# Heads of odd units change sides in the values' products, and the first two experts are picked by early counts

## The chip, the cores and the metric

The kernel runs on one core of one Trainium2 chip. The metric is the device time of one execution in microseconds; the median of three runs is compared. Five engines work side by side: TensorE (matrix products; "PE" in the rows, "PEld" for its weight loads), VectorE ("DVE"), ScalarE ("ACT"), GpSimd ("POOL") and SyncE ("SP", which here only sends DMAs). A "q" behind an engine's name means its instruction queue.

## The reference

Three layers follow each other on 2304 tokens (4 batches of 576) of width 512.

```python
# attention, 8 heads of 64: a down-sampled branch over groups of 4 tokens, and a local band
out_d  = softmax(q4 @ k4.T / 8) @ v4            # q4, k4, v4: means over 4 tokens
out_up = repeat(out_d, 4)
mask   = abs(i - j) < 4
x = out_up + softmax(where(mask, q @ k.T / 8, -1e9)) @ v
# gated layer, d_ff 1536
x = (silu(x @ w_gate) * (x @ w_val)) @ w_out
# 8 experts, d_ff 1024: each token goes to one
e = argmax(cosine(x, expert_emb) / tau);  p = softmax(...)[e]
out = p * (relu(x @ w1[e]) @ w2[e])
```

## The kernel before

**Order.** The kernel is written as some hundred generator tasks. A planner in Python (`Sched`) runs them at build time: each `yield op(engine, ns, priority)` asks for an engine for an estimated time, `wait` and `get` wait for events and buffers, and the planner picks by priority and estimated time which task emits its instructions next. What comes out is a fixed instruction order per engine. Priorities are constants (`HEAD_P`, `WEIGHT_P`, `ROW_P`, ...); `LAT` is the time that the planner allows from one engine to the next.

**Attention.** Work goes by head pairs n = 0 to 15 (batch b = n // 4). The two heads of a pair lie in partitions 0 to 63 and 64 to 127. A sequence is cut into NU = 10 units of UQ = 58 queries; a unit's band needs 64 keys. Pairs 0 to 3 take tasks of their own (`local_e`, `down_e`, `piece_e`). Pairs 4 to 15 take `scores` (band scores, unit u of head h2 into bank `lp[h2]`, even units in the lower and odd units in the upper 64 partitions), `local` (softmax), and `values`: transposes of the weights, the down-sampled product into `av`, then 20 products of 64x64 by 64x58, one for each unit and head, into two banks, 464 columns into the first. `up` is a copy of `av`; VectorE adds `up` to the products into x32, at chunk borders and at the bank's end. With f32 operands each such product stands as two records in the trace.

**Gated layer.** x32 holds chunks of 256 tokens in NX = 3 buffers; `x_split` cuts each into a high and a low part, and products are done in three parts (high by high, high by low, low by high). Chunks are worked on in order 0 to 8; 2 and 3, and 4 and 5, go together.

**Routing.** After a chunk's last product, `route_rows` and `first_rows` multiply its rows by the eight expert rows on VectorE, `route` finds the expert of each token and its place among that expert's tokens, with the counts so far in `base`; `route_base` adds the chunk's counts. GpSimd scatters token numbers into a table in memory (`tab`).

**Experts.** Each expert has a fixed number of slots by its place in the order (`CAPS`; 336 slots are three tiles of 128, 128 and 80). Expert 0 always comes first (`FIXED = 1`); its weights are loaded once the products of chunk 7 are issued, and its first 256 slots are filled from chunks 0 to 7. The others are ranked by their final counts (`last_base`), after chunk 8, and their numbers are loaded into registers from `ordi` (`set_order`, line 1460); `load_experts`, `load_slots` (line 1699: table, line 1720: gather) and `load_groups` (gathers from the third expert on) wait for "turns". Should an expert have more tokens than slots, a block at the end of the kernel handles the rest.

```python
            if e == FIXED:
                yield ("wait", "turns")
```

## Time and profile before

| what | before |
|---|---|
| median of 3 runs | 811.74 us (811.62 to 813.75) |
| profiled execution | 808.81 us, its span 807.2 us |
| TensorE busy | 789.4 us (98%) |
| VectorE busy | 563.2 us (70%) |
| ScalarE busy | 369.1 us (46%) |
| GpSimd busy | 195.1 us (24%) |
| mean granted TensorE clock | 0.997 |

The profiled execution is one run of its own; its span goes from the first to the last instruction. Matmuls are pipelined, so a record's time is longer than the distance to the next one, and the distance of starts tells the pace. Records in one row of the timeline are merged.

### The profile page before, as it was taken

Reading aid. Unit: us, or ns where it says so; the run is one execution under the profiler, and the core shown is the slowest. Engines: PE = TensorE matmul, PEld = TensorE weight load, DVE = VectorE, ACT = ScalarE, POOL = GpSimd, SP = SyncE. Lnnn points to the kernel's source line nnn. Section 1 sums busy time; section 2 is a strip of 40 time slices with the busy share of each in tenths; the row PEclk is TensorE's granted clock in tenths of the full one; section 3 lists DMA queues with packets and bytes.
Section 4 is the critical chain, followed back from the end, with each engine's and each line's share of the span. In section 5 each row is a group of like instructions: output and inputs, shape, how many; then the busy total and the mean of one; then the engine's idle time right before and its main releaser. Section 6 shows DMA issues by size and latency. Waiting matters only on the chain. (4 is left out here: it accounts for less than half of the span.)

```text
span 807.2 us, 16215 instructions
## 1 busy us (share of the span) xinstructions
PE 789.4 (98%) x6122; PEld 691.1 (86%) x6128; DVE 563.2 (70%) x1472; ACT 369.1 (46%) x919; POOL 195.1 (24%) x208
## 2 busy tenths in 40 slices
PE   8989999999999999999999999999989999999997
PEld 5778778877877877877899999999979999999996
DVE  5899889768755468656399997675568778657620
ACT  3887788662332261232241312335345555545531
POOL 5533300010000010000013312012357163555201
PEclk9999999999999999999999999999999999999999
DMA  8995255512201112201143010052189666676401
GB/s 248 283 285 169 63 202 183 166 66 88 75 1 61 62 65 88 75 1 61 67 131 62 19 41 1 27 149 87 29 237 275 217 198 189 180 221 191 156 14 42
DMA packets 64371, 96.35 MB, mean 119 GB/s; under 512 B 15085, under 2 KB 34031, under 8 KB 64160
## 3 DMA queue, kind: packets, MB, share of 16 engines
q1 hardware_dynamic: 59424, 85.50, 34.9%
q0 software_dynamic: 4576, 9.51, 4.0%
q8 instruction: 49, 0.80, 0.4%
q14 instruction: 34, 0.28, 0.1%
q10 hardware_dynamic: 288, 0.26, 0.1%
HBM read 85.42 MB, written 10.29 MB: 119 GB/s over the span
## 5 line engine op out<-in xcount | busy, mean ns | idle before, releaser
L1176 PE MATMUL ps<-xb,w 128*128 128x512 f32 x512 | 171.9, 398 | 0.0
L1120 PE MATMUL ps<-xb,w 128*128 128x256 f32 x960 | 128.1, 285 | 0.3 <-ACT w L726 0.3
L1120 PEld LDWEIGHTS ps<-xb,w 128*128 128x128 f32 x960 | 121.8, 191 | 2.2 <-ACT w L726 0.5
L1176 PEld LDWEIGHTS ps<-xb,w 128*128 128x128 f32 x512 | 96.1, 188 | 22.4 <-issue 0.8
L1851 PE MATMUL ps<-xh,w 128*128 128x288 f32 (+4 forms) x512 | 111.2, 299 | 0.2
L1176 PE MATMUL ps<-xl,w 128*128 128x512 f32 x256 | 100.6, 393 | 0.0
L1851 PEld LDWEIGHTS ps<-xh,w 128*128 128x128 f32 x512 | 84.9, 188 | 1.2 <-ACT sg L1921 1.0
L1647 DVE TENSOR_TENSOR w<-w,w 128x1024 fp32r<-128x1024 f32 x64 | 76.6, 1217 | 8.2 <-ACT w L1644 7.5
L1851 PE MATMUL ps<-xl,w 128*128 128x288 f32 (+4 forms) x256 | 75.9, 296 | 0.0
L1792 POOL DMA_INDIRECT xs<-x2d,w x55 | 64.1, 1166 | 23.0 <-issue 14.3
L1644 ACT CAST w<-w 128x1024 fp32r<-128x1024 f32 x64 | 65.9, 1050 | 0.0
L1835 ACT ACTIVATE eh<-ps 128x288 fp32r<-128x288 f32 (+4 forms) x62 | 26.0, 419 | 83.9 <-PE ps L1851 73.7
L1837 DVE SCALAR_TENSOR_TENSOR el<-ps,eh 128x288 fp32r<-128x288 f32 (+4 forms) x62 | 28.0, 456 | 51.7 <-ACT eh L1835 51.2
L1176 PEld LDWEIGHTS ps<-xl,w 128*128 128x128 f32 x256 | 48.2, 188 | 8.7
L1238 PE MATMUL x<-w,hh 128*128 128x512 f32 x160 | 50.2, 395 | 0.0
L1851 PEld LDWEIGHTS ps<-xl,w 128*128 128x128 f32 x256 | 48.2, 188 | 0.2
L1957 PE MATMUL x<-eh,w 128*128 128x288 f32 (+3 forms) x192 | 46.8, 301 | 0.0
L1957 PE MATMUL ps<-eh,w 128*128 128x288 f32 (+3 forms) x192 | 46.8, 301 | 0.0
L1135 ACT ACTIVATE th<-ps 128x256 f32<-128x256 f32 x64 | 21.1, 380 | 50.8 <-PE ps L1176 50.8
L1150 ACT CAST hh<-th 128x256 fp32r<-128x256 f32 x64 | 24.1, 407 | 39.8 <-DVE th L1144 39.5
L1208 PE MATMUL x<-w,hh 128*128 128x512 f32 x128 | 41.2, 403 | 0.0
L1137 DVE SCALAR_TENSOR_TENSOR th<-th,ps 128x256 f32<-128x256 f32 x64 | 24.1, 415 | 24.5 <-ACT th L1135 24.3
(343 smaller groups left out, 1691.6 us busy)
## 6 DMA issues: line engine op xcount, KB each, us to landing
w<-w SPq DMA_DIRECT2D x64, 512.0 KB
w<-w_gate SPq DMA_DIRECT2D x10, 512.0 KB
w<-w_val SPq DMA_DIRECT2D x10, 512.0 KB
w<-w_out SPq DMA_DIRECT2D x10, 512.0 KB
aw<-qk SPq DMA_DIRECT2D x16, 291.0 KB
x2d<-sg SPq DMA_DIRECT2D x18, 256.0 KB
w<-qk SPq DMA_DIRECT2D x12, 291.0 KB
xl<-x2d SPq DMA_DIRECT2D x13, 256.0 KB
```

The costliest lines, as they stand in the source:

```text
L1120: nc.tensor.matmul(ps[:, o:o + CT], ww[:, k, fs], xx[:, k, :], start=(k == 0 and n == 0), stop=(k == KD - 1 and n == 2))
L1137: nc.vector.scalar_tensor_tensor(out=th, in0=th, scalar=1.0, in1=pg[:, r], op0=ALU.add, op1=ALU.mult)
L1176: nc.tensor.matmul(ps, ww[:, k, fs], xx[:, :, k], start=(k == 0 and n == 0), stop=(k == KD - 1 and n == 2))
L1208: nc.tensor.matmul(x2p[x], l, r[:, js], start=(u == 0 and n == 0), stop=(u == 2 * NFB - 1 and n == 2))
L1238: nc.tensor.matmul(x2p[c, m], l[:, j, ms], r[:, js], start=(p == 0 and j == 0 and n == 0), stop=(p == NFB - 1 and j == 1 and n == 2))
L1644: nc.scalar.copy(hi.bitcast(F32R), raw)
L1647: nc.vector.tensor_tensor(out=lo.bitcast(F32R), in0=raw, in1=hi.bitcast(F32R), op=ALU.subtract)
L1792: nc.gpsimd.indirect_dma_start(out=xs[:, n * P:(n + 1) * P], out_offset=None, in_=x2d.rearrange("t (a d) -> (t a) d", a=KD), in_offset=bas ...
L1835: nc.scalar.activation(hh[:, j, 0:n].bitcast(F32R), ps[:, 0:n], AF.Relu)
L1837: nc.vector.scalar_tensor_tensor(out=hl[:, j, 0:n].bitcast(F32R), in0=ps[:, 0:n], scalar=0.0, in1=hh[:, j, 0:n].bitcast(F32R), op0=ALU.max ...
L1851: nc.tensor.matmul(ps[:, 0:n], ww[:, k, fs], xx[:, k, 0:n], start=(k == 0 and t == 0), stop=(k == KD - 1 and t == 2))
L1957: nc.tensor.matmul(ys[d][:, 0:n], ww, h, start=(f == 0 and t == 0), stop=(f == NF2 - 1 and t == 2))
```

## The change

Three things change. In `scores`, odd units of the two heads go to the other bank, so that in the weights' transposes odd units have the heads' rows swapped; V's odd units are swapped to fit in the layout on the host (pairs 4 to 15). In `values` a product of an odd unit then reads the other half of the rows than it writes of the columns, and the products of even units go to one bank and those of odd units to the other. x32 becomes one ring of three chunks, into which VectorE adds by bank, in the pieces that `runs` gives; `up` is written with each column twice.

The first two experts are picked by `pick`: the one with the highest count behind chunk 6, and behind chunk 7 the highest of the others. `set_one` loads their numbers into registers on SyncE and GpSimd. The other six are ranked after chunk 8 as before. The second place has 312 slots in place of 336.

All priorities and latencies of the planner are new.

```diff
 EARLY = 256
-FIXED = 1
-CAPS = (CAP, CAP, 312, 304, 288, 288, 288, 256)
+CAPS = (CAP, 312, 312, 304, 288, 288, 288, 256)
 SLTE = [tuple(m for m in (P, P, n - 2 * P) if m) for n in CAPS]
...
 NT18 = NTOK // P
-NRK = E - FIXED
+NRK = E
 NCST = P + P // 2 + NPAIR * WK // 2 + 3 * E + 4 * NT18 + NOV + NRK
...
 DMA_T = 700.0
-ACT_P, XP_P, ROW_P, FIRST_P = -0.456, 0.525, -0.154, 30.295
+ACT_P, XP_P, ROW_P, FIRST_P = -0.496, 0.501, 3.222, -1.474
 NX = 3
...
 
-    LAT = {"PE": 210.0, "DVE": 158.0, "ACT": 178.0, "POOL": 143.0}
-    LAT_DMA = 4951.0
+    LAT = {"PE": 210.0, "DVE": 196.0, "ACT": 216.0, "POOL": 181.0}
+    LAT_DMA = 4954.0
     ENTER, LEAVE = 90.0, 240.0
...
 
-HEAD_P = [-2.038, -0.549, -1.624, -1.708, 2.951, 3.075, 1.758, 4.264, 14.859, 18.007, 17.102, 19.186, 33.984, 40.93, 39.946, 38.167]
+HEAD_P = [-3.109, 0.648, -2.052, -1.667, 2.606, 4.218, 1.43, 4.125, 17.975, 14.873, 18.249, 18.867, 37.092, 43.121, 42.894, 40.716]
 NE = 8
...
 NV = 4
-REST_P = [-0.295, -0.252, 0.316, 2.344]
-HALF_P = [0.379, -1.498, 1.707, 0.836]
-VALUE_P = 0.832
-PART_P = [-0.851, 0.298, 0.473]
-CONST_P = 7.293
-TAB_P = 13.08
-EN_P = 0.425
+REST_P = [0.348, 0.116, 0.229, 4.192]
+HALF_P = [-5.803, -4.869, 2.17, 0.149]
+VALUE_P = 1.151
+PART_P = [-0.006, 0.163, 0.799]
+CONST_P = 6.238
+TAB_P = 10.974
+EN_P = 1.384
 EN_T = 0.0
...
 UH = NU // 2
-WEIGHT_P = [1.273, 2.395, 4.193, 0.175, -6.884, 9.779]
+WEIGHT_P = [1.883, 3.305, 7.321, 0.411, -8.772, 3.174]
 
...
     ordi = cst.tile([P, NRK], I32, name="ordi")
-    nc.gpsimd.memset(cape, float(CAP))
+    one = cst.tile([P, 4], F32, name="one")
+    onei = cst.tile([P, 2], I32, name="onei")
+    floor = cst.tile([P, E], F32, name="floor")
 
...
     left = [6 * NFB]
-    slots("x32", atp, NX, [P, KD, CT], True)
+    ring = atp.tile([P, KD, NX * CT], F32, name="ring")
+    for i in range(NX):
+        sc.slots["x32"].append((0.0, ring[:, :, i * CT:(i + 1) * CT]))
     slots("xl2", atp, 1, [P, 2 * KD * CT], True)
...
             t0 = unit0(u)
-            for h2, s in enumerate(lp):
-                nc.tensor.matmul(s[(u % 2) * 64:(u % 2) * 64 + 64, u // 2 * WK:(u // 2 + 1) * WK],
+            for h2 in range(2):
+                nc.tensor.matmul(lp[(h2 + u) % 2][(u % 2) * 64:(u % 2) * 64 + 64, u // 2 * WK:(u // 2 + 1) * WK],
                                  sq[row(h2), t0:t0 + 64], sk[row(h2), t0:t0 + WK], start=True, stop=True)
...
         eT = sk[:GH, 0:4 * G].rearrange("p (h g) -> p h g", h=2)
-        up = sq[:, SP6 + 2 * G:SP6 + 3 * G]
-        xa, xb = yield from pget(2)
-        av = xb[:, 256:256 + G]
+        up = sq[:, SP6:SP6 + 2 * G]
+        xp = yield from pget(2)
+        av = xp[1][:, NPAIR * UQ + 10:NPAIR * UQ + 10 + G]
         yield ("lag", SLACK)
-        yield op("PE", 490 + 20 * 52 + 90, None, "s")
+        yield op("PE", 490 + 10 * 64 + 90, None, "s")
         for kh in range(2):
...
                                  start=(kh == 0), stop=(kh == 1))
-        cut = 8 * UQ
         for u in range(NU):
...
             i = u // 2 * P % 256 + u % 2 * 64
-            xp, q = (xa, UQ * u) if UQ * u < cut else (xb, UQ * u - cut)
+            q = u // 2 * UQ
             for h2 in range(2):
-                r = slice(h2 * D, (h2 + 1) * D)
-                nc.tensor.matmul(xp[r, q:q + UQ - o], sv[r, u * D:(u + 1) * D], T[u // 4][r, i + o:i + UQ], start=True, stop=True)
-        eng = yield psum(G)
-        copy[eng](up, av)
-        t0 = 0
-        while t0 < S:
-            c, o = divmod(b * S + t0, CT)
-            e = min(S, t0 + CT - o, cut if t0 < cut else S)
-            xp, q = (xa, t0) if t0 < cut else (xb, t0 - cut)
-            yield op("DVE", t_dve(e - t0), -1.0)
-            nc.vector.tensor_tensor(
-                out=x32[c][:, hp, o:o + e - t0].rearrange("p (g f) -> p g f", f=4),
-                in0=xp[:, q:q + e - t0].rearrange("p (g f) -> p g f", f=4),
-                in1=up[:, t0 // 4:e // 4].unsqueeze(2).to_broadcast([P, (e - t0) // 4, 4]), op=ALU.add)
-            x_left[c, hp] -= e - t0
+                r, d = ((h2 + u) % 2 * D, h2 * D)
+                nc.tensor.matmul(xp[u % 2][d:d + D, q:q + UQ - o], sv[r:r + D, u * D:(u + 1) * D], T[u // 4][r:r + D, i + o:i + UQ],
+                                 start=True, stop=True)
+        eng = yield psum(2 * G)
+        copy[eng](up.rearrange("p (g f) -> p g f", f=2), av.unsqueeze(2).to_broadcast([P, G, 2]))
+        for e in range(2):
+            for m, us, t0, t1 in runs(b, e):
+                k = (t1 - t0) // 2
+                at_ = (b * S + t0) % (NX * CT)
+                yield op("DVE", t_dve(2 * m * k), -1.0)
+                nc.vector.tensor_tensor(
+                    out=ap_of(ring, (hp * NX * CT + at_), [[2 * UQ, m], [2, k], [1, 2]]),
+                    in0=ap_of(xp[e], us // 2 * UQ + t0 - UQ * us, [[UQ, m], [2, k], [1, 2]]),
+                    in1=ap_of(up, t0 // 2, [[UQ, m], [1, k], [0, 2]]), op=ALU.add)
+            if e == 0:
+                pput(xp[0])
+        pput(xp[1])
+        for c in range(b * S // CT, (b * S + S - 1) // CT + 1):
+            x_left[c, hp] -= min(b * S + S, (c + 1) * CT) - max(b * S, c * CT)
             if x_left[c, hp] == 0:
                 sc.set(("xr", c, hp))
-            if e in (cut, S):
-                pput(xa if e == cut else xb)
-            t0 = e
         sc.set(("done", n))
+
+    def runs(b, e):
+
+        cut = -(b * S) % (NX * CT)
+        got = []
+        for u in range(e, NU, 2):
+            t0, t1 = UQ * u, min(UQ * (u + 1), S)
+            for a, z in ((t0, min(t1, cut)), (max(t0, cut), t1)) if t0 < cut < t1 else ((t0, t1),):
+                if got and a == t0 and z - a == UQ and got[-1][3] - got[-1][2] == UQ and not (got[-1][2] < cut <= a):
+                    got[-1][0] += 1
+                else:
+                    got.append([1, u, a, z])
+        return got
 
...
         for c in range(NCHUNK):
-            x32[c] = yield ("get", "x32")
+            yield ("get", "x32")
+            x32[c] = ring[:, :, c % NX * CT:(c % NX + 1) * CT]
             sc.set(("x32", c))
...
         nc.vector.tensor_tensor(out=base, in0=base, in1=base0, op=ALU.subtract)
-        r0, lo = iota8[:, 0, 0:NRK], iota8[:, 0, FIXED:]
+        r0 = lo = iota8[:, 0, :]
         key, rank, val = rk[:, 0], rk[:, 1], rk[:, 2]
...
         yield op("DVE", 75, -0.9, True)
-        nc.vector.scalar_tensor_tensor(out=key, in0=lo, scalar=-1.0 / 16, in1=base[:, FIXED:], op0=ALU.mult, op1=ALU.add)
+        nc.vector.scalar_tensor_tensor(out=key, in0=lo, scalar=-1.0 / 16, in1=base, op0=ALU.mult, op1=ALU.add)
+        yield op("DVE", 75, -0.9, True)
+        nc.vector.tensor_tensor(out=key, in0=key, in1=rk[:, 3], op=ALU.add)
         yield op("DVE", 110, -0.9, True)
...
         yield op("DVE", 100, -0.8)
-        nc.vector.tensor_reduce(out=cape[:, FIXED:], in_=rk2, axis=AX.X, op=ALU.add)
+        nc.vector.tensor_reduce(out=cape, in_=rk2, axis=AX.X, op=ALU.add)
         yield op("DVE", 75, -0.8, True)
...
         yield ("lag", 500)
-        for i in range(NRK):
-            on_ = [mybir.EngineType.SP] + ([mybir.EngineType.Pool] if FIXED + i == 1 else [])
-            turn[FIXED + i] = nc.values_load(ordi[0:1, i:i + 1], engines=on_, min_val=FIXED, max_val=E - 1,
-                                             skip_runtime_bounds_check_because="a permutation of the ranked experts")
+        for i in range(2, E):
+            turn[i] = nc.values_load(ordi[0:1, i:i + 1], engines=[mybir.EngineType.SP], min_val=0, max_val=E - 1,
+                                     skip_runtime_bounds_check_because="a permutation of the ranked experts")
         sc.set("turns")
...
 
-        return x[e] if e < FIXED else x[bass.ds(turn[e], 1)].rearrange("o r c -> (o r) c")
+        return x[bass.ds(turn[e], 1)].rearrange("o r c -> (o r) c")
 
...
 
-            yield op("DVE", 75, -0.9)
-            nc.vector.tensor_scalar(out=base[:, 0:1], in0=base[:, 0:1], scalar1=float(EARLY), scalar2=None, op0=ALU.max)
+            yield ("wait", "picked")
+            yield op("DVE", 75, -0.9, True)
+            nc.vector.tensor_tensor(out=base, in0=base, in1=floor, op=ALU.max)
+        if c >= NCHUNK - 3:
+            sc.spawn(sc.cur.prio, pick(c - NCHUNK + 3))
         sc.set(("base", c))
+
+    def pick(i):
+
+        key, up_, got = rk[:, 0], rk[:, 2], rk[:, 3]
+        lo = iota8[:, 0, :]
+        yield op("DVE", 75, -0.7, True)
+        nc.vector.tensor_tensor(out=key, in0=base, in1=base0, op=ALU.subtract)
+        yield op("DVE", 75, -0.7, True)
+        nc.vector.scalar_tensor_tensor(out=key, in0=lo, scalar=-1.0 / 16, in1=key, op0=ALU.mult, op1=ALU.add)
+        if i == 1:
+            yield op("DVE", 75, -0.7, True)
+            nc.vector.tensor_tensor(out=key, in0=key, in1=got, op=ALU.subtract)
+        yield op("DVE", 80, -0.7)
+        nc.vector.tensor_reduce(out=one[:, i:i + 1], in_=key, axis=AX.X, op=ALU.max)
+        yield op("DVE", 75, -0.7, True)
+        nc.vector.tensor_scalar(out=up_, in0=key, scalar1=one[:, i:i + 1], scalar2=None, op0=ALU.is_equal)
+        yield op("DVE", 75, -0.7, True)
+        nc.vector.tensor_tensor(out=key, in0=up_, in1=lo, op=ALU.mult)
+        yield op("DVE", 80, -0.7)
+        nc.vector.tensor_reduce(out=one[:, 2 + i:3 + i], in_=key, axis=AX.X, op=ALU.add)
+        yield op("DVE", 75, -0.7, True)
+        nc.vector.tensor_copy(onei[:, i:i + 1], one[:, 2 + i:3 + i])
+        sc.set(("one", i))
+        if i == 0:
+            yield op("DVE", 75, -0.7, True)
+            nc.vector.scalar_tensor_tensor(out=floor, in0=up_, scalar=float(EARLY), in1=base0, op0=ALU.mult, op1=ALU.add)
+            yield op("DVE", 75, -0.7, True)
+            nc.vector.tensor_scalar(out=got, in0=up_, scalar1=8192.0, scalar2=None, op0=ALU.mult)
+            sc.set("picked")
+        else:
+            yield op("DVE", 75, -0.7, True)
+            nc.vector.scalar_tensor_tensor(out=got, in0=up_, scalar=4096.0, in1=got, op0=ALU.mult, op1=ALU.add)
+
+    def set_one(i):
+
+        yield ("wait", ("one", i))
+        yield ("lag", 500)
+        turn[i] = nc.values_load(onei[0:1, i:i + 1], engines=[mybir.EngineType.SP, mybir.EngineType.Pool], min_val=0, max_val=E - 1,
+                                 skip_runtime_bounds_check_because="the place of a maximum among the experts")
+        sc.set(("turn", i))
 
...
         for e in range(E):
-            if e == FIXED:
-                yield ("wait", "turns")
+            yield ("wait", ("turn", e) if e < 2 else "turns")
             for nm, dst in (("w1", w1s), ("w2", w2s)):
...
         js = slice(parts[0], parts[-1] + 1)
-        if e >= FIXED:
-            yield ("wait", "turns")
+        yield ("wait", ("turn", e) if e < 2 else "turns")
         for t in range(2):
...
 
-        if e > 2:
+        if e > 3:
             yield ("wait", ("xs", e - 2, 0))
...
         sc.spawn(NCHUNK * 10 + 3, turn_slots(), 0.0)
+        for i in range(2):
+            sc.spawn(NCHUNK * 10 + 3, set_one(i), 0.0)
         sc.spawn(NCHUNK * 10 + 3, set_order(), 0.0)
...
              t.reshape(P, -1).view(np.float32), np.tile(EARLY + P * np.arange(NOV, dtype=np.float32), (P, 1)),
-             np.tile(np.array(CAPS[FIXED:], np.float32), (P, 1))]
+             np.tile(np.array(CAPS, np.float32), (P, 1))]
     return {"cst": np.concatenate(parts, axis=1), "tri": np.triu(np.ones((P, P), np.float32), 1),
...
     vw = np.stack([vp[..., unit0(u):unit0(u) + WK, :] for u in range(NU)], axis=4)
+    late = vw.reshape(B * HP, 2, WK, NU, D)[NV:]
+    late[:, :, :, 1::2] = late[:, ::-1, :, 1::2].copy()
     arr["vw"] = np.ascontiguousarray(vw).reshape(B, HP, P, NU * D)
```

## Rows read from the trace of the kernel before

**Rows 1.** The page: busy time of each engine, share of the span, instructions.
```profile
PE   789.4 (98%) x6122; PEld 691.1 (86%) x6128; DVE 563.2 (70%) x1472; ACT 369.1 (46%) x919; POOL 195.1 (24%) x208
```

**Rows 2.** Windows: length, busy time by engine, PEclk, DMA share, GB/s.
```profile
52.00:130.00 78.00, 76.74 (x737) 65.13 (x736) 70.05 (x158) 62.54 (x159) 19.96 (x16) 0.98 0.51 161
130.00:400.00 270.00, 270.00 (x1873) 215.38 (x1872) 176.05 (x442) 104.89 (x321) 11.63 (x16) 1.00 0.23 75
400.00:500.00 100.00, 100.00 (x694) 93.53 (x693) 90.72 (x378) 28.26 (x79) 24.65 (x26) 1.00 0.20 51
604.00:808.00 204.00, 196.96 (x1398) 191.66 (x1396) 122.50 (x197) 98.37 (x165) 83.50 (x72) 0.99 0.55 168
```

**Rows 3.** Waits of TensorE: total us, times, longest.
```profile
PE ps L1731 <- DMA xs<-x2d,tb: 2.9, 2, 1.7
PE ps L847 <- DVE x L933: 1.5, 1, 1.5
```

**Rows 4.** Windows around the pause at 47 us, columns as in rows 2.
```profile
47.00:51.00 4.00, 1.16 (x30) 0.90 (x25) 4.00 (x12) 3.59 (x9) 0.00 (x0) 1.00 0.53 134
51.00:55.00 4.00, 4.00 (x37) 3.69 (x38) 3.29 (x7) 3.13 (x13) 3.68 (x3) 0.57 1.01 292
```

**Rows 5.** Timeline of TensorE, a `values` block, first and last row of three.
```profile
98.35 0.68 PE L980 MATMUL ps<-w 64*64 64x58 f32 x16
...
99.32 0.40 PE L980 MATMUL ps<-w 64*64 64x58 f32 x8
```

**Rows 6.** Timeline of TensorE, a `scores` block.
```profile
94.70 0.81 PE L700 MATMUL ps<-w,w 64*64 64x64 f32 x40
```

**Rows 7.** Line 989, additions into x: ns min/median/max, first and last start.
```profile
L989 DVE TENSOR_TENSOR x<-ps,w x16: 161/306/417, 66.0 to 127.3; 128x192 f32<-128x192 f32 x4, 128x256 f32<-128x256 f32 x4, 128x16 f32<-128x16 f32 x4, 128x112 f32<-128x112 f32 x4
```

**Rows 8.** Timeline of TensorE, first layer of the second and third expert.
```profile
603.63 0.32 PE L1851 MATMUL ps<-xl,w 128*128 128x336 f32 x1
...
605.02 0.32 PE L1851 MATMUL ps<-xl,w 128*128 128x336 f32 x1
...
653.10 0.30 PE L1851 MATMUL ps<-xl,w 128*128 128x312 f32 x1
...
654.38 0.31 PE L1851 MATMUL ps<-xl,w 128*128 128x312 f32 x1
```

**Rows 9.** Timeline of VectorE, counts added behind chunks 6 and 7.
```profile
496.22 0.35 DVE L1599 TENSOR_TENSOR base<-base,ps 128x8 f32<-128x8 f32 x2
...
534.26 0.35 DVE L1599 TENSOR_TENSOR base<-base,ps 128x8 f32<-128x8 f32 x2
```

**Rows 10.** Timeline of SyncE's DMA issues.
```profile
514.14 1.68 SPq L1610 DMA_DIRECT2D x2d<-sg  x2
524.84 10.81 SPq L1663 DMA_DIRECT2D w<-w  x4
...
585.09 2.99 SPq L1663 DMA_DIRECT2D w<-w  x4
588.32 1.22 SPq L1666 DMA_DIRECT2D w<-w  x1
```

**Rows 11.** Line 1460, register loads of the order: ns min/median/max, first and last start.
```profile
L1460 POOLq TENSOR_LOAD <-ordi x1: 498/498/498, 580.1 to 580.1; - x1
```

**Rows 12.** Timeline of GpSimd around the first expert's last table load.
```profile
574.67 1.79 POOL L1387 DMA_INDIRECT tab<-cn,si  x1 [0.48 <-DVE base L1378]
...
581.19 0.57 POOL L1699 DMA_DIRECT2D tb<-tab  x1 [4.12 <-DVE cape L1442]
```

**Rows 13.** DMA issues by line, median us from issue to landing.
```profile
tab<-cn,si POOLq DMA_INDIRECT x18, 3.3
```

**Rows 14.** A window at the gathers, columns as in rows 2.
```profile
592.00:596.00 4.00, 2.01 (x12) 1.53 (x12) 1.17 (x2) 1.53 (x2) 1.23 (x2) 1.00 1.06 357
```

**Rows 15.** Line 1483, row products: ns min/median/max, first and last start.
```profile
L1483 DVE SCALAR_TENSOR_TENSOR ps<-xl,aw x52: 678/698/702, 411.4 to 490.8; 128x512 f32<-128x512 f32 x52
```

## Prediction

> **What bounds the kernel now.** I read the page first. TensorE is busy for 789.4 of 807.2 us [rows 1], so 17.8 us are idle, and the kernel can get shorter in two ways only: TensorE has less to do, or it waits less. The windows by stage say where which holds. From 130 to 500 us it is busy without a break, while VectorE has slack up to 400 us (176 of 270 us) and next to none from 400 to 500 us (90.7 of 100) [rows 2]. Between 52 and 130 us TensorE is busy for 76.7 of 78 us and VectorE for 70.1, so there they run nearly level [rows 2]. The waits of TensorE name the idle time: the largest, 2.9 us in two pieces, is for gathered rows of an expert, and the start holds several of 1 to 1.5 us [rows 3]. One of these pauses costs twice. Of 47 to 51 us TensorE works only 1.16 us, and right behind it, from 51 to 55 us, the granted clock reads 0.57, that is mostly the lower level of 1.2 GHz [rows 4]. Those 4 us lose 4 x 0.43 = 1.7 us of work beside the 2.8 us of pause.
>
> **The values' products.** The change removes no product of `values`: each of the 12 late heads (B*HP = 16, less NV = 4) keeps 20 of them, 40 records in the trace. It moves half of them to the two quarters that stood idle. Before, head 0 uses rows and columns 0 to 63 and head 1 uses 64 to 127, so two quarters work. The timeline has one such block from 98.35 us to 99.32 + 0.40 = 99.72, so 1.37 us for 40 records of 58 columns [rows 5]. The nearest row with four quarters is `scores` in the same kernel: 40 records of 64 columns take 0.81 us [rows 6]. It differs in what it multiplies, not in type or tile, and its result banks are also split so that the two row halves under one column half write different banks, as the new line does with xp[u % 2]. Hence 1.37 - 0.81 = 0.56 us a head, or 12 x 0.56 = 6.7 us. If the time goes with the columns, it is 0.81 x 58/64 = 0.73, a gain of 0.64 a head and 7.7 us; if the quarters do not help, 0. I take 0.56, since the scores' row is the same kind of instruction. Four of the heads (b = 1) run between 64 and 127 us, where VectorE is nearly full; I let half of their 2.2 us be lost to it. **-5.6 us.**
>
> A page of the Trainium skill speaks against this gain: "TensorEngine Tiling (Array Packing)", section Instruction Overhead, says that a matmul costs some 60 cycles however few columns it has, and that one should not tile on a dimension that is already small. At 2.4 GHz that is an estimate of 25 ns a record, which would leave about 0.17 us a head and 2 us in all. The scores' block does not bear it out for these records, with 0.81 us for 40 of them, or 20 ns each [rows 6].
>
> The new bank choice in `scores` changes neither the number of its products nor the quarters that they use: 0. The swap of V's odd units is done in the layout of the input, on the host: the same bytes are loaded.
>
> **Taking the products out of PSUM.** The copy of the down-sampled part grows from 144 to 288 columns (written twice, in pairs). The additions into x are now cut by bank and by the ring's end and not by chunk: by `runs`, 7 pieces for b = 1 and 2 and 3 for b = 3, so 4 x (7 + 7 + 3) = 68 for the 48 of before, over the same 576 columns. An addition takes 161 ns for 16 columns and 417 for 256 [rows 7], so 1.07 ns a column and 0.144 us fixed. Twenty more are 20 x 0.144 = 2.9 us of VectorE, and the copies at that slope 12 x 144 x 1.07 = 1.8 us. The work that hides it is TensorE's own unbroken row of products from 130 to 400 us [rows 2], where 8 of the 12 heads are. The inner runs of two elements are not in the trace; a plain run is the nearest row. I take 0; at worst the part before 130 us, 4 x 3 x 0.144 + 0.6 = 2.3 us, lands on TensorE.
>
> **24 columns less.** The expert in second place gets 312 slots and not 336. Its two layers have 8 x 4 x 3 = 96 products each, 192, all streaming the slots, so 64 groups of three. Three groups of 336 go from 603.63 to 605.02 us, 0.463 each; three of 312 from 653.10 to 654.38, 0.427 [rows 8]. 64 x 0.036 = **-2.3 us**, on TensorE, which does not wait there (196.96 of 204 us busy from 604 us on, and nearly all the rest is the tail after the last product) [rows 2]. I see no bound far from it.
>
> **Picks instead of a fixed first and a late second expert.** `pick` adds some 20 small VectorE instructions, two register loads on SyncE and two on GpSimd. The first pick follows chunk 6's counts, which are complete at 496.22 us [rows 9]; the first expert's weights are asked for at 524.84 us [rows 10]. So the new wait has 28 us of room. Behind the load on SyncE stand chunk 7's stores, which start at 514.14 us [rows 10], and on GpSimd nothing but that chunk's own steps. The second pick follows chunk 7's counts, at 534.26 us [rows 9]; behind its load on GpSimd stand the first expert's table loads, which wait for chunk 7's scatters anyway. Before, GpSimd's load of the order register stands at 580.1 us [rows 11], and the second table load of the first expert is queued behind it: it sits idle for 4.12 us and starts at 581.19 [rows 12]. That load also needs the scatter of 574.67 us to land, 3.3 us after issue by the median [rows 12, 13], so about 578. With the register long loaded, the tables and the gathers behind them move up by some 3 us. Five weight loads of the second expert, sent from 585.09 us on, right beside these gathers [rows 10], move ahead of them as well, since they now wait only for buffers; the DMA engines were full (1.06) from 592 to 596 us [rows 14]. TensorE's two waits there, 2.9 us [rows 3], should mostly go: at most -2.9, at least 0 if the gathers meet the early loads instead. I take **-2.3 us**. Registers in the addresses of the first expert's 8 loads cost SyncE issue time only.
>
> **Priorities.** All of the planner's priorities and its latencies (158 to 196 ns for VectorE, and so on) are new, so the order of instructions shifts everywhere. The rows price this at the start alone: the pause at 47 to 51 us with its low clock is 2.8 + 1.7 = 4.5 us [rows 4]. It may go, and one like it may come: 0, with 4.5 us to either side.
>
> **Sum.** -5.6 - 2.3 - 2.3 = -10.2 us on the profiled 808.81 us (807.2 of span and 1.6 around it) gives 798.6. The median of the runs is 811.74, 2.9 above the profiled one; the same step from there gives **801.5 us**.
>
> **Rivals.**
> (a) The quarters bring nothing: the pace of the products is set by something else than the quarters' own streams, such as loading V's tiles. For it: the values' records are fewer columns wide than any other group. Against it: the scores' 0.81 us. Time: 811.74 - 4.6 = 807.1; by the page's 25 ns it would be 805. Chance 0.08.
> (b) The start comes out with one more pause of the kind at 47 to 51 us, and the gather's wait stays: -5.6 - 2.3 + 4.5 = -3.4, so 808.3. Chance 0.10.
> (c) The start loses its pause too: -10.2 - 4.5, so 797.0. Chance 0.17.
> (d) Slower: VectorE falls behind with the routing rows. Each of the 96 row products takes about 0.8 us, they now rank at 3.222 behind nearly all else, and from 400 to 500 us VectorE is 91% busy [rows 2]. Then chunk 6's counts come late, and with them the first expert's weights. It decides once the counts slip by the 28 us of room, less the 6 us by which TensorE comes sooner, and by the gain of 10 us beyond: 35 us late, say, is a pause of 13 us before the experts and 814.5. Against it: before the change the backlog is done at 491 us [rows 15], and 32 of the 128 products have their own task, which moves up (FIRST_P from 30.3 to -1.5). Chance 0.06.
> (e) The change does not do what it says because a picked expert overflows its slots, so that the block at the end runs: two weights of 2 MB each at the 357 GB/s of the fullest window [rows 14] are 12 us alone, and with tables, gather and scatter at 3 to 5 us each some 25, so about 826. From the reference's inputs I count 329 tokens for the leading expert (336 slots) and 296 for the second (312), so it should not. Chance 0.02.
>
> **How the numbers follow.** The forecast (799 to 804 us) has 0.57, the rivals 0.08, 0.10, 0.17, 0.06 and 0.02. Leaving out (d), (e) and the far halves of (b) and (c) gives 796.5 to 809 us for 8 in 10. A change of this kernel can be told from none at about 0.3%, 2.4 us. Faster holds the forecast, (c), most of (a) and half of (b): 0.85. Same, from (a) and (b): 0.07. Slower, from (d) and (e): 0.08.
>
> **What would show it.** Each values block takes about 0.8 us, not 1.37. The second expert's groups of three start 0.43 us apart. GpSimd's register loads stand near 500 and 535 us, no table load waits behind one at 580 us, and TensorE's wait for gathered rows is under 1 us. VectorE's additions into x number 68 plus those of the early heads, without a wait of TensorE on them. It would be wrong if a values block stayed above 1 us, if a new pause stood before 60 us or between 85 and 130 us, or if TensorE waited for the first expert's weights after its last product of the gated layer.

## The result and the profile after

The changed kernel takes 802.5 us (median of 4, 800.98 to 807.49) against 812.75 us of the kernel before in the same series (median of 4, 811.62 to 814.24): ratio 0.9883, 95% interval 0.9836 to 0.9931. Two further series of it, told below, gave 0.9891 (0.9854 to 0.9927) and 0.9884 (0.9833 to 0.9935). So the change is worth 1.1 to 1.2%, or 8.8 to 9.5 us of 811.74; the medians themselves lie 10.3 to 11.7 us apart in the three series. The forecast was 801.5 us, that is -10.2. The profiled execution took 802.39 us (before: 808.81), its span is 800.8 us.

The page of the changed kernel, as [rows 1]:

```profile
PE 785.2 (98%) x6123; PEld 682.8 (85%) x6129; DVE 559.8 (70%) x1498; ACT 369.9 (46%) x920; POOL 209.5 (26%) x219
```

TensorE is busy for 4.2 us less while the span is 6.4 us shorter, so it has less to do and does not wait more. VectorE has 26 more instructions and no more work.

The timeline of TensorE, one block of `values` (now line 982), against [rows 5]:

```profile
96.80 0.46 PE L982 MATMUL ps<-w 64*64 64x58 f32 x16
...
97.31 0.29 PE L982 MATMUL ps<-w 64*64 64x58 f32 x8
```

From 96.80 to 97.31 + 0.29 = 97.60 it is 0.80 us, where it was 1.37. That is the length of the `scores` block [rows 6], and the 11 other blocks look the same.

The first layer of the second expert, against the groups of 336 columns in [rows 8]:

```profile
599.78 0.30 PE L1910 MATMUL ps<-xl,w 128*128 128x312 f32 x1
...
600.63 0.31 PE L1910 MATMUL ps<-xl,w 128*128 128x312 f32 x1
```

These are the first and the last of three groups; the groups are 0.425 us apart, not 0.463. The waits of TensorE (total, times, longest), against [rows 3]:

```profile
PE x L2016 <- issue: 2.0, 6, 0.4
...
PE ps L1790 <- DMA xs<-x2d,tb: 1.1, 2, 0.6
```

The wait for gathered rows (line 1731 before, 1790 now) has shrunk from 2.9 to 1.1 us, just above the 1 us that the prediction names. The wait on top is new, and it has no releaser: "issue" is time in which the engine waited for nothing that the profile shows. Windows at that place, columns as in [rows 2]:

```profile
600.00:604.00 4.00, 3.35 (x21) 2.83 (x20) 1.73 (x4) 0.43 (x1) 3.09 (x4) 1.00 0.58 185
604.00:608.00 4.00, 2.54 (x7) 1.37 (x7) 0.00 (x0) 0.31 (x1) 1.56 (x2) 0.73 0.14 36
608.00:612.00 4.00, 4.00 (x13) 2.86 (x12) 3.79 (x8) 2.32 (x4) 0.00 (x0) 0.50 0.64 139
```

And the timeline of TensorE inside them:

```profile
603.37 0.39 PE L2016 MATMUL x<-eh,w 128*128 128x312 f32 x1 [0.42 <-issue]
604.08 0.30 PE L2016 MATMUL x<-el,w 128*128 128x312 f32 x1 [0.32 <-issue]
604.80 0.41 PE L2016 MATMUL x<-eh,w 128*128 128x312 f32 x1 [0.41 <-issue]
```

Products that start 0.14 us apart elsewhere start 0.7 us apart here, seven times in a row. Behind them the granted clock reads 0.50, the lower level of 1.2 GHz. I call this the slow stretch; what it costs follows from a second profile of the same kernel that has none (below).

The other signs that the prediction named. VectorE's additions into x, by line:

```profile
L991 DVE TENSOR_TENSOR ring<-ps,aw x40: 171/208/461, 181.1 to 396.5; 128x174 f32<-128x174 f32 x8, 128x58 f32<-128x58 f32 x8, 128x54 f32<-128x54 f32 x8, 128x36 f32<-128x36 f32 x4
L991 DVE TENSOR_TENSOR ring<-ps,w x28: 160/206/333, 62.0 to 113.8; 128x116 f32<-128x116 f32 x8, 128x174 f32<-128x174 f32 x4, 128x58 f32<-128x58 f32 x4, 128x18 f32<-128x18 f32 x4
```

There are 68, as counted. GpSimd's register loads of the picks stand at 504.5 and 530.0 us, and none behind the order:

```profile
L1664 POOLq TENSOR_LOAD <-onei x2: 303/402/501, 504.5 to 530.0; - x2
```

The stretch in which VectorE was nearly level with TensorE, and the pause at 47 us, against [rows 2, 4]:

```profile
52.00:130.00 78.00, 76.99 (x710) 64.39 (x709) 72.48 (x174) 65.95 (x161) 20.37 (x17) 1.00 0.57 188
...
47.00:51.00 4.00, 2.87 (x58) 2.44 (x59) 3.99 (x9) 3.46 (x12) 2.75 (x3) 1.00 0.59 185
51.00:55.00 4.00, 4.00 (x44) 3.58 (x40) 3.40 (x9) 3.38 (x12) 2.67 (x3) 1.00 0.92 253
```

VectorE works 2.4 us more between 52 and 130 us (70.05 before), and TensorE's idle time there still falls from 1.26 to 1.01 us. The pause at 47 us has shrunk from 2.84 to 1.13 us of idle time in this execution, and no low clock follows it.

### The profile page after: what moved, and what is told of

It reads as the page before. It is cut to its first block, busy times and chain, and to the rows that moved or that the text cites. A ratio compares the mean times of both kernels' runs of the same rounds, so it can differ in the third digit from the quotient of the medians.

```text
span 800.8 us, 16291 instructions
## 1 busy us (share of the span) xinstructions
PE 785.2 (98%) x6123; PEld 682.8 (85%) x6129; DVE 559.8 (70%) x1498; ACT 369.9 (46%) x920; POOL 209.5 (26%) x219
## 5 line engine op out<-in xcount | busy, mean ns | idle before, releaser
L1193 PE MATMUL ps<-xb,w 128*128 128x512 f32 x512 | 174.7, 400 | 0.0
L1910 PE MATMUL ps<-xh,w 128*128 128x288 f32 (+3 forms) x512 | 109.6, 297 | 0.1
L1910 PE MATMUL ps<-xl,w 128*128 128x288 f32 (+3 forms) x256 | 75.5, 295 | 0.0
L1851 POOL DMA_INDIRECT xs<-x2d,w x55 | 68.4, 1243 | 23.4 <-issue 15.8
L1896 DVE SCALAR_TENSOR_TENSOR el<-ps,eh 128x288 fp32r<-128x288 f32 (+3 forms) x62 | 28.0, 453 | 58.3 <-ACT eh L1894 49.4
L1894 ACT ACTIVATE eh<-ps 128x288 fp32r<-128x288 f32 (+3 forms) x62 | 25.8, 417 | 81.1 <-PE ps L1910 44.3
L2016 PE MATMUL x<-eh,w 128*128 128x288 f32 (+2 forms) x192 | 47.1, 302 | 1.4 <-issue 1.4
L2016 PE MATMUL ps<-eh,w 128*128 128x288 f32 (+2 forms) x192 | 46.9, 302 | 0.1
L1094 ACT CAST hh<-th 128x256 fp32r<-128x256 f32 x44 | 17.8, 407 | 54.2 <-DVE th L1091 53.6
L1167 ACT CAST hh<-th 128x256 fp32r<-128x256 f32 x64 | 24.1, 407 | 37.9 <-DVE th L1161 37.8
```

The lines of the kernel that those rows point to most:

```text
L1193: nc.tensor.matmul(ps, ww[:, k, fs], xx[:, :, k], start=(k == 0 and n == 0), stop=(k == KD - 1 and n == 2))
L1851: nc.gpsimd.indirect_dma_start(out=xs[:, n * P:(n + 1) * P], out_offset=None, in_=x2d.rearrange("t (a d) -> (t a) d", a=KD), in_offset=bas ...
L1894: nc.scalar.activation(hh[:, j, 0:n].bitcast(F32R), ps[:, 0:n], AF.Relu)
L1896: nc.vector.scalar_tensor_tensor(out=hl[:, j, 0:n].bitcast(F32R), in0=ps[:, 0:n], scalar=0.0, in1=hh[:, j, 0:n].bitcast(F32R), op0=ALU.max ...
L1910: nc.tensor.matmul(ps[:, 0:n], ww[:, k, fs], xx[:, k, 0:n], start=(k == 0 and t == 0), stop=(k == KD - 1 and t == 2))
L2016: nc.tensor.matmul(ys[d][:, 0:n], ww, h, start=(f == 0 and t == 0), stop=(f == NF2 - 1 and t == 2))
```

## The experiments

My theory was the sum on record: quarters, columns and the early second pick each bring what their rows say, and the new priorities nothing of their own. The rivals were that the new order brings the gain, and that the early pick's gain is given back. Twelve kernels ran, in three series of four; the ratios are to the kernel before in the same series.

| run | median us (runs) | ratio | 95% interval |
|---|---|---|---|
| e1 values in two quarters | 804.29 (6) | 0.9909 | 0.9880 to 0.9937 |
| e2 old priorities | 812.12 (12) | 1.0008 | 0.9989 to 1.0026 |
| e3 second expert known late | 800.54 (6) | 0.9864 | 0.9838 to 0.9891 |
| e4 the changed kernel | 799.90 (6) | 0.9891 | 0.9854 to 0.9927 |
| f1 old priorities, new WEIGHT_P | 814.79 (12) | 1.0018 | 0.9988 to 1.0048 |
| f2 kernel before, new priorities | 841.68 (6) | 1.0349 | 1.0304 to 1.0393 |
| f3 second place 336 | 807.75 (10) | 0.9906 | 0.9872 to 0.9940 |
| f4 only WEIGHT_P old | 807.13 (7) | 0.9903 | 0.9867 to 0.9940 |
| g1 tables early, weights late | 802.89 (6) | 0.9856 | 0.9810 to 0.9901 |
| g2 splits behind the tables | 805.13 (6) | 0.9886 | 0.9838 to 0.9934 |
| g3 the changed kernel | 804.72 (6) | 0.9884 | 0.9833 to 0.9935 |
| g4 as e3 | 802.88 (6) | 0.9865 | 0.9808 to 0.9921 |

The kernel before took 811.57, 813.4 and 816.24 us (medians of 17, 22 and 11) in the three series, so times are compared within a series or by ratio.

**The changed kernel again (e4).** No edit.

> The changed kernel once more, for the pause of TensorE at 603 to 611 us: products that start 0.7 us apart, without a wait that the profile shows, and a low clock behind it, 6 us in all. Theory (the pause belongs to this execution): the profile shows none there, or one elsewhere, and the time is 796 to 798 us where none stands. Rival (it belongs to the program): it stands at the same product again.

Four of its six executions took 799.3 to 800.4 us, two 805.5 and 806.6. The profiled one (799.41) has no slow stretch. The products of the experts' second layers in it, and in the changed kernel's first profile, by line (last columns: first and last start):

```profile
L2016 PE MATMUL ps<-eh,w x192: 289/298/309, 605.3 to 770.6; 128*128 128x288 f32 x96, 128*128 128x312 f32 x64, 128*128 128x304 f32 x32
```
```profile
L2016 PE MATMUL ps<-eh,w x192: 289/298/462, 601.8 to 773.5; 128*128 128x288 f32 x96, 128*128 128x312 f32 x64, 128*128 128x304 f32 x32
```

The same instructions in the same order take 165.3 us in one and 171.7 us in the other. The slow stretch costs 6.4 us in this execution, which is about the distance between the two groups of e4's times; the two longer executions of e4 were not profiled. In the third profile of the same kernel (g3) it costs 4.6 us, by the table at the end of this section.

**The quarters alone (e1).** The odd units' heads stay on their own side; all else, the order too, is the changed kernel's.

```diff
-                nc.tensor.matmul(lp[(h2 + u) % 2][...
+                nc.tensor.matmul(lp[h2][...
-                r, d = ((h2 + u) % 2 * D, h2 * D)
+                r, d = (h2 * D, h2 * D)
-    late[:, :, :, 1::2] = late[:, ::-1, :, 1::2].copy()
```

> The changed kernel with the heads of odd units left on their own side, in the weights, in V's layout and in the products; banks, pieces, plan and the order of all instructions stay as changed. Theory (the quarters give the gain): each values block takes 1.37 us again and not 0.80, and the kernel is 12 x 0.57 = 6.8 us slower than the changed one, some 4 us faster than before. Rival 1 (the two banks give the gain, not the quarters): a block stays near 0.8 us and the time does not change. Rival 2 (TensorE's saving is lost to VectorE): blocks are longer, but the whole is less than 3 us slower than the changed one.

Timeline of TensorE, the first and the last of the eight late blocks, in e1:

```profile
190.34 0.68 PE L982 MATMUL ps<-aw 64*64 64x58 f32 x16
...
191.32 0.40 PE L982 MATMUL ps<-aw 64*64 64x58 f32 x8
...
408.94 0.68 PE L982 MATMUL ps<-aw 64*64 64x58 f32 x16
```

and the starts of the same two in e4:

```profile
183.34 0.46 PE L982 MATMUL ps<-aw 64*64 64x58 f32 x16
...
398.03 0.46 PE L982 MATMUL ps<-aw 64*64 64x58 f32 x16
```

A block takes 191.72 - 190.34 = 1.38 us again. From the first to the last of the eight, seven blocks' worth, e1 needs 218.60 us and e4 214.69: 3.91 us, or 0.56 a head. Every bit of the block's gain reaches the path there. The totals can't resolve it: e1's median is 4.4 us above e4's, its ratio 0.0018 (1.5 us) above, and the intervals overlap. The trace decides: from 130 to 400 us TensorE is busy for 270.00 of 270 us in both. It also says why the totals do not. TensorE's first block of `values` and GpSimd's last scatter stand in e1 at

```profile
67.31 1.11 PE L982 MATMUL ps<-w 64*64 64x58 f32 x16
...
581.33 1.00 POOL L1404 DMA_INDIRECT tab<-cn,si  x1 [0.30 <-DVE si L1392]
```

and in e4 at

```profile
62.17 0.70 PE L982 MATMUL ps<-w 64*64 64x58 f32 x16
...
569.86 1.00 POOL L1404 DMA_INDIRECT tab<-cn,si  x1 [0.30 <-DVE si L1392]
```

From the one to the other e1 takes 514.02 us and e4 507.69: 6.3 us more, of the 12 x 0.57 = 6.8 that were expected, and behind the last scatter both take 228 us to the end. But e1 also reaches its first block 5.1 us later, behind a wait of 1.8 us without a releaser at 29 us and a granted clock of 0.50 to 0.62 from 28 to 40 us. What the start loses or wins in an execution is nearly as large as what the quarters bring.

**The priorities (e2, f1, f2, f4).** e2 is the changed kernel with all the priorities and latencies of the kernel before, f1 the same but with the new WEIGHT_P, f4 the changed kernel with only WEIGHT_P old. f2 is the kernel before with all of the new ones.

```diff
-HEAD_P = [-3.109, 0.648, -2.052, ...
+HEAD_P = [-2.038, -0.549, -1.624, ...
-WEIGHT_P = [1.883, 3.305, 7.321, 0.411, -8.772, 3.174]
+WEIGHT_P = [1.273, 2.395, 4.193, 0.175, -6.884, 9.779]
...
-    LAT = {"PE": 210.0, "DVE": 196.0, "ACT": 216.0, "POOL": 181.0}
+    LAT = {"PE": 210.0, "DVE": 158.0, "ACT": 178.0, "POOL": 143.0}
```

> The changed kernel with all priorities and latencies of the planner as before. Theory (priorities matter at the start alone, by some 3 us): the pause of TensorE before 60 us comes back, with 2 to 5 us, and the kernel is 2 to 5 us slower than the changed one. Rival 1 (priorities carry most of the gain): 7 us slower or more. Rival 2 (they carry none): within 1.5 us of the changed one.

> The changed kernel with the old priorities and latencies, but with the new WEIGHT_P (the ranks of the six blocks of gated-layer weights in the queue for decoding). The run with all the old priorities had no gain and one pause of TensorE of 9.2 us at 134 us, behind the decoding of a block of w_out. If the pause comes from the ranks of the weights alone, it goes here and the time falls by about the 9.2 us and the low clock behind it, to 800 to 803 us. If it comes from the whole set of ranks (heads against weights, chunks against both), the time stays between 807 and 813.

> The kernel before with the new priorities and latencies and nothing else. If the new set is better by itself, this is 4 to 10 us faster than before, 802 to 808 us. If the set only fits the new code (its own durations and buffers) as the old set fitted the old code, it gains nothing, and a pause of some us may come somewhere before 160 us: 811 to 822.

> The changed kernel with the old WEIGHT_P alone, all other priorities new. If the ranks of the weights make the pause near 134 us, it comes here as well: 808 to 812 us. If they matter only together with the heads' ranks, 799 to 803.

The old priorities with the new code take the whole gain away (e2). The top wait of TensorE in e2, then in f2 (f1 has the same one, of 10.5 us):

```profile
PE x L1225 <- ACT w L492: 9.2, 1, 9.2
```
```profile
PE x L1208 <- ACT w L489: 23.7, 1, 23.7
```

It is one pause at one place, the gated layer's first use of a w_out block that ScalarE has not decoded yet. By line, e2's decoding and its first use of w_out:

```profile
L492 ACT CAST w<-w x30: 637/660/692, 31.5 to 144.8; 128x512 fp32r<-128x512 f32 x30
L1225 PE MATMUL x<-w,hh x128: 387/393/796, 109.1 to 416.0; 128*128 128x512 f32 x128
```

and e4's:

```profile
L492 ACT CAST w<-w x30: 634/662/696, 28.2 to 137.4; 128x512 fp32r<-128x512 f32 x30
L1225 PE MATMUL x<-w,hh x128: 387/393/501, 114.9 to 402.5; 128*128 128x512 f32 x128
```

In e2 TensorE comes to w_out 5.8 us sooner and the decoding ends 7.4 us later, on a VectorE and a ScalarE that are shared with the heads. The order is fixed, so the products stand and wait, and the clock falls behind the pause. A window of e2:

```profile
130.00:150.00 20.00, 10.75 (x41) 8.10 (x40) 14.87 (x29) 16.19 (x28) 0.73 (x1) 0.74 0.53 184
```

In f4 TensorE is busy for all 20 us of that window, at a clock of 1.00. f1 and f4 say that the ranks of the weights are not the cause by themselves: with the new ones alone the pause stays, with the old ones alone it does not come. f4's 0.9903 can't be told from the changed kernel's. f2 says that the new set is no better in itself: with the old code it is 3.5% slower. Each set fits the code that it came with. What a set planned anew for the old code would gain was not tried, so these runs do not say how much of the change new priorities alone could bring.

**24 columns (f3).**

```diff
-CAPS = (CAP, 312, 312, 304, 288, 288, 288, 256)
+CAPS = (CAP, CAP, 312, 304, 288, 288, 288, 256)
```

> The changed kernel with 336 slots in second place again. The products stream 24 more columns in 64 groups of three: 64 x 0.036 = 2.3 us more if that is all, 802.2 us against 799.9 of the changed kernel. If the order behind it shifts for good or ill, another amount; if the second expert waits for its gathers anyway, less than 1 us.

Timeline of TensorE in f3:

```profile
600.00 0.32 PE L1910 MATMUL ps<-xl,w 128*128 128x336 f32 x1
...
600.93 0.32 PE L1910 MATMUL ps<-xl,w 128*128 128x336 f32 x1
```

Two groups of three take 0.93 us, 0.465 each, against 0.425: 64 x 0.040 = 2.6 us. The ratio is 0.0015 to 0.0023 above the changed kernel's three, so 1.2 to 1.9 us, with an interval that holds zero as well.

**The early second pick (e3, g4, g1, g2).** In e3 and g4 the second expert's number comes from the final order, for weights and tables. In g1 only its weights wait for that order, in g2 nothing does, but VectorE's splits of its weights wait until its tables are joined.

```diff
 # e3, g4, in set_one
-        yield ("wait", ("one", i))
+        yield ("wait", ("one", i) if i == 0 else "order")
-        turn[i] = nc.values_load(onei[0:1, i:i + 1], ...
+        turn[i] = nc.values_load((onei if i == 0 else ordi)[0:1, i:i + 1], ...
 # g1, in load_experts
-            yield ("wait", ("turn", e) if e < 2 else "turns")
+            yield ("wait", ("turn", e) if e < 1 else "turns")
 # g2, in split_w, ahead of VectorE's instruction
+        if key[1] == 1:
+            yield ("wait", ("tb", 1, 0))
```

> The changed kernel with the second expert's number loaded from the final order, behind chunk 8, as before; the first pick stays early. Theory (the early second pick saves the waits for gathered rows): GpSimd's register load stands in front of the tables again, TensorE waits for gathered rows some 3 us and not 1.1, and the kernel is 1.5 to 2.5 us slower. Rival (the early weights of the second expert keep VectorE so busy that the gathers come no sooner, counted from chunk 8's last product): less than 1 us slower. The pause of TensorE near 603 us in the changed kernel's profile may go with it, if the load of weights and rows brought it about: then the kernel is some 4 us faster.

> The changed kernel with the second expert's number from the final order for weights and tables alike, beside the others on one chip. By the prediction's term it should be 2.3 us slower than the changed kernel; by the first look at it (800.5 against 799.9 us), within 1 us of it, though TensorE's wait for gathered rows is 2.8 us against 1.1.

> The changed kernel with the second expert's weights asked for only behind the final order, as before, while its number still goes to GpSimd early for the table loads. If the early weights are what took the early tables' gain back (eight splits of 1.2 us each on VectorE between 570 and 582 us, in front of the AND of the tables), the AND comes within 2 us of the tables' landing here, the gathers start 4 to 5 us sooner than in the changed kernel, TensorE's wait for gathered rows falls from 1.1 us to 0.3 us or less, and the time is 1 us below that of the changed kernel, unless the second expert then waits for its weights. If the early second pick has no worth in either part, the gathers stay where they are and the time too.

> The changed kernel in which VectorE's splits of the second expert's weights wait until its tables are joined, so that weights and tables are both early and only the order on VectorE differs. By the theory that the splits hold up the tables: gathers at about 577 us instead of 582 against the same start, TensorE's wait for gathered rows under 0.3 us, 1 us off the total. By the rival, that the gathers wait for the transfers around them and not for VectorE, the wait stays near 1 us. If the splits come too late instead, TensorE waits for a weight of the second expert near 592 us.

> The changed kernel as it is, on the same chip as the other three: 799 to 803 us, and now and then 6 us more.

First what the early pick does in the changed kernel. GpSimd's timeline, against [rows 12]:

```profile
566.29 1.00 POOL L1404 DMA_INDIRECT tab<-cn,si  x1 [0.30 <-issue]
568.07 1.22 POOL L1758 DMA_DIRECT2D tb<-tab  x2 [0.78 <-DMA tab<-cn,si]
569.84 1.53 POOL L1758 DMA_DIRECT2D tb<-tab  x2 [0.55 <-issue]
577.29 1.05 POOL L1779 DMA_INDIRECT xs<-x2d,tb  x1 [5.91 <-DVE rk L1457]
```

The table loads follow the last scatter at once, with no 4 us of idle time between them. But the gather behind them now waits 5.91 us for VectorE, whose timeline (chosen rows) is:

```profile
575.71 1.22 DVE L1708 TENSOR_TENSOR w<-w,w 128x1024 fp32r<-128x1024 f32 x1
576.84 0.16 DVE L1764 TENSOR_TENSOR tb<-tb 128x4 int32<-128x4 int32 x1
```

Line 1764 joins the tables; ahead of it stand seven splits of weights (line 1708) since 566.81 us, 1.22 us each. Three of them, the first expert's, stand in g1 and g2 too; the other four are the second's, and g1 and g2 take them away in two ways, and agree. GpSimd's timeline in g1, then in g2 (whose lines are 2 further down):

```profile
570.65 1.00 POOL L1404 DMA_INDIRECT tab<-cn,si  x1 [0.30 <-DVE si L1392]
...
579.21 1.05 POOL L1779 DMA_INDIRECT xs<-x2d,tb  x1 [3.05 <-DVE tb L1764]
```
```profile
569.19 0.98 POOL L1404 DMA_INDIRECT tab<-cn,si  x1 [0.30 <-issue]
...
577.75 2.51 POOL L1781 DMA_INDIRECT xs<-x2d,tb  x1 [3.49 <-DVE tb L1766]
```

From the last scatter to the first gather it is 8.6 us in both, against 11.0 in the changed kernel and, from 574.67 us [rows 12] to the first gather, 9.5 in the kernel before:

```profile
584.20 1.05 POOL L1720 DMA_INDIRECT xs<-x2d,tb  x1 [0.30 <-issue]
```

So the splits did hold the gathers up, by 2.4 us, not by the 4 to 5 that I expected. TensorE's wait for gathered rows is then below 1 us in g1 and absent in g2, where it is 2.8 and 3.0 us in e3 and g4. But the times do not follow it: 0.9864 and 0.9865 with the longest wait, 0.9886 with none. g1 says where part goes, in the waits of TensorE:

```profile
PE ps L1910 <- DVE xl L1797: 1.1, 1, 1.1
PE ps L1790 <- issue: 0.9, 1, 0.9
```

What comes sooner at the gather is waited for at the next step. In g2 it is the slow stretch, with 2.5 us of waits without a releaser in the second expert's first layer (line 1912).

The three runs with the second expert's weights late have ratios of 0.9856 to 0.9865, the four with them early 0.9883 to 0.9891, some 2 us more. Each pair of intervals overlaps, so the totals decide nothing here.

The traces separate what the totals mix. GpSimd's last scatter is in [rows 12] for the kernel before; its second layers' products (first and last start, as above), then scatter and products in e3 and in g4:

```profile
L1957 PE MATMUL ps<-eh,w x192: 289/298/322, 612.5 to 780.0; 128*128 128x288 f32 x96, 128*128 128x336 f32 x32, 128*128 128x312 f32 x32, 128*128 128x304 f32 x32
```

```profile
568.64 1.00 POOL L1404 DMA_INDIRECT tab<-cn,si  x1 [0.30 <-DVE si L1392]
L2016 PE MATMUL ps<-eh,w x192: 289/298/310, 607.2 to 773.1; 128*128 128x288 f32 x96, 128*128 128x312 f32 x64, 128*128 128x304 f32 x32
```
```profile
566.89 1.00 POOL L1404 DMA_INDIRECT tab<-cn,si  x1 [0.30 <-DVE si L1392]
L2016 PE MATMUL ps<-eh,w x192: 289/298/310, 606.9 to 772.7; 128*128 128x288 f32 x96, 128*128 128x312 f32 x64, 128*128 128x304 f32 x32
```

From the start of the last scatter to the last start of these products, in the kernel before and in every profile with all of the changed kernel's priorities and 312 slots in second place:

| profile | second expert's tables | its weights | slow stretch | us |
|---|---|---|---|---|
| before | late | late | no | 205.3; 202.7 less the 2.6 for 24 columns (f3) |
| e4, e1 | early | early | no | 200.7, 200.7 |
| g1 | early | late | no | 202.4 |
| e3, g4 | late | late | no | 204.4, 205.8 |
| g3, the first profile | early | early | yes | 205.3, 207.2 |
| g2 | early | early, splits behind the tables | yes | 206.1 |

So in an execution without the slow stretch the early second pick does save time on TensorE's path: 2.0 us against the kernel before, columns apart, and 3.7 to 5.1 us against e3 and g4. The slow stretch costs 4.6 and 6.5 us, more than that. Windows at the gathers, columns as in [rows 2], in e3, g4 and e4:

```profile
580.00:592.00 12.00, 9.22 (x45) 7.25 (x45) 5.19 (x15) 3.14 (x6) 5.73 (x6) 0.90 0.98 288
```
```profile
580.00:592.00 12.00, 8.97 (x41) 7.19 (x40) 4.91 (x11) 4.28 (x7) 5.52 (x6) 0.80 0.95 289
```
```profile
580.00:592.00 12.00, 10.90 (x68) 9.14 (x67) 8.51 (x27) 4.79 (x8) 6.51 (x5) 1.00 0.45 106
```

With the weights late, their transfers run beside the gathers (DMA share 0.98 and 0.95, against 0.45), TensorE idles 2.8 and 3.0 us instead of 1.1, and the granted clock falls behind these waits. Each line of the table rests on one or two executions.

## Why the prediction was right, and where it was not

**The quarters: right, and a little too careful.** The block fell to 0.80 us, so by 0.57 where 0.56 was taken from the scores' row. e1 shows it whole on the path for the late heads. For b = 1 I let half of 2.2 us go to VectorE. From the first block of b = 1 to the last scatter e1 is 6.3 us longer than e4, of 6.8 in full, though in both the first of these blocks stands at a low clock. So most of it arrived, and the term is -6.3 rather than -5.6. The estimate by columns (0.73 us) did not hold: 58 columns take the time of 64. Rival (a) is refuted.

The Trainium skill, "TensorEngine Tiling (Array Packing)", section Instruction Overhead, would have left about 1.0 us a block by its 60 cycles (an estimate: 40 x 25 ns at 2.4 GHz). The trace has 0.80 us, and from the first start to the 33rd 97.31 - 96.80 = 0.51 us, 16 ns a record, so here the measurement decides against the figure. The 0.17 us a head that the prediction draws from that page does not follow from 1.37 - 1.0 = 0.37, which would be 4.4 us in all; 0.17 comes out only with some 0.2 us for the end of the last record, which it does not say. The same page, section Restrictions and Gotchas, says that row tiles may not access one PSUM bank at the same time; the quarters without the split of the banks were not tried for that reason, and no run here shows it.

**The additions at no cost: right.** They are 68, and the 2.4 us that VectorE works more between 52 and 130 us are the 2.3 named as the bound. They stayed hidden in this execution, by TensorE's idle time there.

**24 columns: right.** -2.3 was predicted; the distance of the groups gives -2.6, the totals 1.2 to 1.9 without deciding.

**The early second pick: the size about right, half of the way to it wrong, and a cost missing.** The half that failed is "the tables and the gathers behind them move up by some 3 us". The tables did move up, the gathers did not: they start 11.0 us behind the last scatter, where it was 9.5 before. The step named the weight loads that move ahead and asked whether their transfers would meet the gathers; it left out VectorE's splits, which come with those weights and stand in VectorE's fixed order ahead of the tables' AND. That kept 2.4 us. The half that held is that the weight loads "move ahead of them as well": with the transfers out of the way TensorE's wait falls from 2.9 to 1.1 us. In an execution without the slow stretch the term of -2.3 is thus about right, 2.0 us from the last scatter on. What the prediction left out is the slow stretch, which stands in most profiles with those weights early and in none with them late, and takes more than the gain where it comes. Against e3 and g4, whose waits are long and have a low clock behind them, the totals show neither a gain nor a loss.

**The priorities: the zero is not shown, and the bound was wrong.** No run prices the new order by itself between two sets that each fit their code. I priced the order by the start alone, at 4.5 us to either side. A set that does not fit loses 12 us by the medians (e2 against e4; 9.5 by the ratios) or 28 us (f2) at a place that I had not named, the decoding of w_out between 110 and 150 us. The new priorities are thus a needed part of the change: with the old ones it is worth nothing.

**The sum.** By the runs it is -6.3 for the quarters, -2.6 for the columns and -2.0 for the second pick, -10.9 in an execution without the slow stretch; where it comes it adds 4.6 to 6.5, which leaves -4.4 to -6.3. e4's four shorter executions lie 11.2 to 12.3 us below the kernel before in its series (811.57), its two longer ones 4.9 and 6.1. The forecast of -10.2 holds for executions of the first kind. That the median of the first four runs, one of which is profiled with the slow stretch, still came within 1 us of it is in part luck, since what the start loses differs by several us from execution to execution. Rivals (b) and (c) were about the start: its pause at 47 us is mostly gone in the first profile, but e4 has one at 58 to 62 us (2.52 of 4 us busy) with a clock of 0.50 behind it, one of the signs that were named against the prediction, so the start gained little for certain. (d) did not come: the first expert's weights are asked for at 516.35 us, 8.5 sooner than in [rows 10]. Nor did (e).

**Open.** Why the slow stretch comes in some executions, and whether the early weights bring it about; they go together in these profiles, and no run shows a cause.

## What to carry to other kernels

When small products leave quarters of the array idle, price the gain from a block in the same kernel that already uses all quarters, not from columns or cycles. After a change to durations or buffers in a kernel with a planned order, plan the priorities anew before judging it: the old ones hid all of this gain behind one pause at a shared decoder. When a transfer is moved ahead, look at what it brings along on the other engines. And where two versions have the same total, compare the distance between two events that both traces have: here a gain of 2 to 5 us and a loss of 5 to 6 us hid each other.

## What the runs showed of the hardware

The slow stretch was not expected: TensorE's products 0.7 us or twice that apart, whether of 312 or of 336 columns, with no releaser in the records, for 2 to 8 us, and behind them, in five of six profiles, a granted clock near 0.50 (f1, the shortest, keeps 1.00). Among the 14 profiles it stands between 600 and 618 us, at the second expert's products, in six of the nine in which that expert's weights are loaded early (the changed kernel's first and third, f1, f3, f4, g2) and in none of the five in which they are loaded late. That is few profiles, and single waits without a releaser stand elsewhere too (1.8 us at 29 us in e1, 1.5 us in f3). It falls on other products each time: in the changed kernel's third profile it runs from 605 to 609 us, in the first from 603 to 607.5.

Its 4.6 to 6.5 us are about the spread of the changed kernel's times in e4.

Records of 64x64 by 64x58 start 16 ns apart on four quarters (0.51 us for 32) and 30 ns apart on two (190.34 to 191.32 us in e1, 32 records).
